# Two layers of recurrent-memory attention and gMLP on one Trainium2 core: part of the last-token projections made during the weight load

## The chip, the cores and the metric

The kernel runs on one core of one Trainium2 chip. The metric is the device time of one execution in microseconds; smaller is better. A run's time is the median of its executions. One execution is recorded by the profiler, and all views below are of that one.

## The reference

```python
def _A_ref(x, mem0, Wq, Wk, Wv, Wo, seg_len):      # 2048 tokens, 512 wide, 32 heads of 128, 8 memory rows, segments of 32
    mem = mem0
    for s in range(n_seg):                          # 64 segments, one after the other
        xs = x[:, s * seg_len:(s + 1) * seg_len, :]
        h = jnp.concatenate([mem, xs], axis=1)      # 40 rows
        q, k, v = h @ Wq, h @ Wk, h @ Wv            # per head
        p = softmax(where(mask, q @ k.T * scale, -1e9))
        o = (p @ v) @ Wo
        mem = o[:, :M, :]                           # the next segment's memory
        outs.append(o[:, M:, :])

def _B_ref(x, w_in, w_sp, b_sp, w_out):             # gMLP, 1376 wide inside, mixes over all 2048 tokens
    z = gelu(x @ w_in); z1, z2 = halves(z); z2 = layernorm(z2)
    return (z1 * (w_sp @ z2 + b_sp)) @ w_out

x = x + A(layernorm(x)); x = x + B(layernorm(x))    # twice: two layers with the same weights
x = x + A(layernorm(x)); x = x + B(layernorm(x))
```

## The kernel before

`a_block` and `b_block` run in turn, twice. The attention is a loop over 64 segments whose memory rows pass from one to the next. Four segments are a tile of 128 tokens; 16 tiles are a layer, and four tiles are a group.

A segment's 40 rows are 8 memory rows and 32 tokens. The program takes 32 of them through the segment's own chain (the 8 memory rows and the first 24 tokens: `psQ`, `psm`, `psK`, `psV` in `segment`), and does the last 8 tokens of the four segments of a tile together, 32 rows, ahead of time: query, key and value of these are the *chunks* of a tile. A chunk j is one half of the heads of Wq (j = 0, 1), Wk (2, 3) or Wv (4, 5): 16 matmuls of 128x512, four at a time in four column strips of the array (`b_mms`). Chunks go by ScalarE to `rowsB` and from there, turned by a transposing DMA on SP's queue or by VectorE (`b_out`), to `QTB` and `KTB`, or to `VB` and over DRAM (`store_v`, `spread_v`) to `VX`. GpSimd's copies in `prep_segment` take the parts of a segment from there.

The work of a chunk is put into the running tile's segments as filler: `segment` calls `fill()` three times, before `pv(0)`, before the Wo matmuls, and while VectorE makes the next memory. Each call takes one step of a generator called `more`:

- in the first four tiles of a layer `b_even` gives the next tile's six chunks as one, one and four times four matmuls a segment;
- later `b_units` gives them in nine steps over the first three segments of a tile (one, two and five times four matmuls), and the fourth segment has `y_part`: the output rows of the last tokens of the group before, 32 matmuls into `pwB`, added to `yB` by VectorE (`adds`). Rows of a whole group are stored by `store_last`.

After the attention of a segment come the output matmuls: `wo_pairs` (heads 0 to 15, two column strips a head, into `px`) and `wo_rest` (heads 16 to 31, four strips a head, into `pw`). VectorE folds `px` into `t1` by way of `cross` (`fold`), adds `pw` and turns the sum into the next segment's `hT` (`build_hA`), which the next `psQ` waits for.

PE, DVE and ACT execute in the order written inside a block (`ORDERED`); the order on SP and GpSimd is chosen by the framework's scheduler.

At the start of the first layer rows of tiles 0 and 1 and the memory are loaded on SP's queue, the weights on GpSimd's, in halves of 2048 columns: Wq and Wk first halves, second halves, Wv, Wo. Meanwhile the chunks of tile 0 and two of tile 1 are made (`units`, `units1`), in this order:

```python
units, units1 = b_units(0, 6), b_units(1, 2, alone=True)
for gen, n in ((units, 4), (units1, 2), (units, 4)):
    for _ in range(n):
        next(gen)
        run(turns)
        run(copies)
    run(turns)
```

The values of tile 0 and the rest of tile 1 are made within segment 0.

## Time and profile before

| | |
|---|---|
| time, median of 3 runs | 1623.56 us (1617.69 to 1624.75) |
| the profiled execution | 1618.1 us, its span 1616.4 us |
| TensorE busy | 1578.8 us, 98% |
| weight loads, VectorE, ScalarE, GpSimd busy | 61%, 66%, 65%, 19% |
| psQ of segments 0 and 1, first layer | 30.45 and 52.75 us |
| first layer's tile 1, tile 5 (four segments) | 38.67 and 40.12 us |
| the first layer's last segment starts | 671.4 us |

Times in the trace are counted from the span's start. A group or a timeline line tells the engine, the program's line, the operation, the tiles (out<-in), the shape and the count, and in brackets how long the engine had been idle before and what released it. `PE` are matmuls and `PEld` the loads of their stationary operand. A busy TensorE says nothing of how fast it ran; the length of equal matmuls and the granted clock do.

### The profile page before, as it was taken

Reading aid. Unit: us, or ns where it says so; the run is one execution under the profiler, and the core shown is the slowest. Engines: PE = TensorE matmul, PEld = TensorE weight load, DVE = VectorE, ACT = ScalarE, POOL = GpSimd, SP = SyncE. Lnnn points to the kernel's source line nnn. Section 1 sums busy time; section 2 is a strip of 40 time slices with the busy share of each in tenths; the row PEclk is TensorE's granted clock in tenths of the full one; section 3 lists DMA queues with packets and bytes.
Section 4 is the critical chain, followed back from the end, with each engine's and each line's share of the span. In section 5 each row is a group of like instructions: output and inputs, shape, how many; then the busy total and the mean of one; then the engine's idle time right before and its main releaser. Section 6 shows DMA issues by size and latency. Waiting matters only on the chain.

```text
span 1616.4 us, 91216 instructions
## 1 busy us (share of the span) xinstructions
PE 1578.8 (98%) x41182; PEld 983.8 (61%) x41182; DVE 1069.0 (66%) x3060; ACT 1048.9 (65%) x2281; POOL 301.6 (19%) x667
## 2 busy tenths in 40 slices
PE   5899999999999999999999999999999999999999
PEld 2566666666666766666656666666666666665565
DVE  3567766667776776784466666666677667768622
ACT  2677777777777777670047777777777777776400
POOL 5111111112211221320011111111122112224000
PEclk9999999999999999999999999999999999999999
DMA  9312121213311332377941112121233223425697
GB/s 357 100 39 46 42 43 43 44 43 85 82 47 43 90 90 70 96 181 166 210 145 44 49 43 51 46 47 47 67 92 77 47 69 99 100 52 175 145 185 171
DMA packets 259805, 148.11 MB, mean 92 GB/s; under 512 B 193752, under 2 KB 235840, under 8 KB 259416
## 3 DMA queue, kind: packets, MB, share of 16 engines
q1 hardware_dynamic: 246184, 98.46, 27.7%
q0 software_dynamic: 13232, 43.82, 8.3%
q8 instruction: 322, 5.28, 1.3%
q14 instruction: 67, 0.55, 0.1%
HBM read 59.68 MB, written 37.19 MB: 60 GB/s over the span
## 4 chain that ended last, share of the span: by engine, by line
PE 55%; DVE 1%; issue 1%; DMA 0%; ACT 0%; POOL 0%; POOLq 0%; DVEq 0%
PE pg L397 9%; PE psQ L714 7%; PE psK L714 7%; PE psb L714 5%; PE pz L296 5%; PE psO L825 3%; PE px L818 3%; PE psV L714 3%; PE psm L714 3%; PE py L440 2%; PE pwB L837 2%; PE psO L1026 2%; PE psT L1018 1%; PE psS L977 1%; PE pw L1285 0%
## 5 line engine op out<-in xcount | busy, mean ns | idle before, releaser
L714 PEld LDWEIGHTS <-hT 128*32 128x32 bf16 x12288 | 344.2, 97 | 266.5 <-DVE hT L926 12.5
L714 PE MATMUL psV<-Wv_sb,hT 128*32 128x512 bf16 x2048 | 165.8, 379 | 0.0
L954 DVE STREAM_TRANSPOSE QQ<-rows 128x256 f32<-128x256 f32 x256 | 113.1, 442 | 78.6 <-ACT rows L951 76.6
L951 ACT CAST rows<-psQ 128x512 bf16<-128x512 f32 x256 | 144.1, 591 | 29.5 <-PE psQ L714 27.3
L1047 DVE TENSOR_TENSOR uT<-psO,Rm 128x128 bf16<-128x128 f32 x256 | 74.6, 291 | 123.4 <-ACT Rm L1044 123.0
L986 ACT ACTIVATE S<-psS 128x224 bf16<-128x224 f32 x256 | 92.2, 360 | 96.9 <-PE psS L981 96.7
L954 DVE STREAM_TRANSPOSE KA<-rows 128x256 f32<-128x256 f32 x256 | 113.5, 443 | 61.7 <-ACT rows L951 58.6
L397 PE MATMUL pg<-z,wspT 128*128 128x344 bf16 x1024 | 154.3, 309 | 0.0
L1050 DVE TENSOR_TENSOR uT<-psO,Rt 128x384 bf16<-128x384 f32 x256 | 140.2, 548 | 18.7 <-ACT Rt L1126 16.4
L714 PE MATMUL psK<-Wv_sb,hT 128*32 128x512 bf16 x2048 | 151.9, 378 | 0.0
L1126 ACT ACTIVATE Rt<-Rt 128x512 f32<-128x512 f32 x256 | 147.3, 622 | 4.1
L714 PE MATMUL psQ<-Wq_sb,hT 128*32 128x512 bf16 x2048 | 136.5, 383 | 7.2 <-DVE hT L926 3.3
L825 PE MATMUL psO<-Wo_high,uT 128*32 128x128 bf16 x8192 | 140.0, 219 | 2.3 <-issue 2.0
L714 PE MATMUL psQ<-Wk_sb,hT 128*32 128x512 bf16 x2048 | 136.8, 383 | 0.0
L714 PE MATMUL psm<-Wq_sb,hT 128*32 128x512 bf16 x2048 | 135.3, 380 | 0.0
L714 PE MATMUL psK<-Wk_sb,hT 128*32 128x512 bf16 x2048 | 134.9, 379 | 0.0
L818 PE MATMUL px<-Wo,uT 128*32 128x256 bf16 x3840 | 133.2, 273 | 0.4
L1123 ACT ACTIVATE Rt<-psT 128x1024 f32<-128x1024 f32 x128 | 131.0, 1024 | 3.1
L397 PEld LDWEIGHTS <-wspT 128*128 128x128 bf16 x1024 | 100.2, 98 | 53.2
L825 PEld LDWEIGHTS <-uT 128*32 128x32 bf16 x8192 | 125.7, 97 | 8.6 <-issue 4.2
L818 PEld LDWEIGHTS <-uT 128*32 128x32 bf16 x4096 | 107.2, 97 | 27.4 <-DVE uT L1047 1.1
L911 POOL COPY KX<-old 128x128 bf16<-128x128 bf16 x128 | 65.3, 539 | 275.4 <-PE psS L981 211.0
(202 smaller groups left out, 2874.5 us busy)
## 6 DMA issues: line engine op xcount, KB each, us to landing
o_d<-o_sb SPq DMA_DIRECT2D x126, 64.0 KB
vb_d<-front SPq DMA_DIRECT2D x30, 256.0 KB
VX<-vb_d SPq DMA_DIRECT2D x120, 64.0 KB
ln_x<-xd SPq DMA_DIRECT2D x26, 256.0 KB
y_o<-o_d POOLq DMA_DIRECT2D x22, 256.0 KB, 3.4
xd<-y_o POOLq DMA_DIRECT2D x22, 256.0 KB, 2.8
Wq_sb<-in_A_Wq_dram POOLq DMA_DIRECT2D x8, 512.0 KB, 10.0
Wk_sb<-in_A_Wk_dram POOLq DMA_DIRECT2D x8, 512.0 KB, 10.4
```

The lines of the kernel that those rows point to most:

```text
L296: nc.tensor.matmul(pz[:, c0:c1], lhsT=xnT[:, kt, :], rhs=w_in_sb[:, kt, c0:c1], start=(kt == 0), stop=(kt == KT - 1))
L397: nc.tensor.matmul(pg[t][:, k, 0:344], lhsT=wsp[t][:, st, :], rhs=z(st, 344 * k, 344 * k + 344), start=(st == 0), stop=(st == NT - 1))
L714: return [nc.tensor.matmul(ps[32 * cg:32 * cg + 32, :], lhsT=lhs(kt, cg), rhs=rhs(kt, cg), start=(kt == 0), stop=(kt == KT - 1), tile_posi ...
L818: nc.tensor.matmul(px[at:at + 32, 0:256], lhsT=lhs[:, h, :], rhs=wo_rhs(h, slice(k + 2, None, -2) if h % 2 else slice(k, None, 2)), start= ...
L825: nc.tensor.matmul(pw[32 * cg:32 * cg + 32, :], lhsT=lhs[:, h, :], rhs=wo_rhs(h, cg), start=False, stop=(h == H - 1), tile_position=(0, 32 ...
L951: return r, mms, copy(r[:].rearrange("p (n el two) -> p n el two", n=8, two=2), ps.rearrange("p (n two el) -> p n el two", n=8, two=2))
L954: nc.vector.transpose(out=(QQ[:, j % 2, :, 0:32] if j < 2 else KA[:, j % 2]).bitcast(F32).rearrange("p n q one -> p n (q one)"), in_=r[:]. ...
L986: return nc.scalar.activation(out=S[:, r], in_=psS[:, r, 0:224], func=ACT.Exp, scale=scale)
L1047: nc.vector.tensor_tensor(out=hview(uT_cur[:], r, 24, 32), in0=oview(r, 0, 8), in1=Rm[:, r].rearrange("p g (n q) -> p g n q", q=8), op=ALU ...
L1050: nc.vector.tensor_tensor(out=hview(uT_nxt[:], r, 0, 24), in0=oview(r, 8, 32), in1=rview(r, 0, 24), op=ALU.mult)
L1123: nc.scalar.activation(out=Rt[:], in_=psT[:], func=ACT.Ln)
L1126: nc.scalar.activation(out=rt, in_=rt, func=ACT.Exp, scale=-1.0)
```

## The change

In the first layer chunks 0 and 2 (first half of the heads' queries and keys) of tiles 8 to 15 are taken out of the loop. The last 8 tokens of their 32 segments are two sets of 128 rows (groups 2 and 3, `EARLY`). The rows are loaded on SP's queue at the start, normalised (`early_norm`, between two steps of `_consts`), turned on TensorE (`early_turn`), and multiplied over the whole array: eight units of eight matmuls of 128x512, each copied to SBUF by ScalarE (`early_units`). The units stand between the chunks of tiles 0 and 1. GpSimd's queue stores the result to DRAM after segment 0 (`early_store`, eight DMAs). In tiles 7 to 14 of the first layer a new filler, `b_light`, gathers the next tile's two chunks by two transposing DMAs from DRAM, and spreads the four chunks left and the output rows (`y_steps`, which `y_part` now uses too) as one, one and four times four matmuls in every segment; chunk 3 is turned by VectorE. `spread_v` is issued a segment later in these tiles. In both layers `wo_pairs` takes heads 0 to 13 and `wo_rest` 14 to 31.

```diff
-WO_PAIR = 16
+WO_PAIR = 14
+EARLY = (2, 3)
+EARLY_CHUNKS = (0, 2)
...
+        for G in EARLY:
+            src = x_in[4 * P * G:4 * P * (G + 1), :].rearrange("(j r) c -> j r c", j=16)
+            nc.sync.dma_start(x_last[G], src[:, SEG - M:SEG])
...
+        def early_norm():
+            MVe, RSe = c["MVe"], c["RSe"]
+            for k, G in enumerate(EARLY):
+                _stats(nc, rp, x_last[G], MVe[:, k, :])
+            _rstd_act(nc, RSe[:], MVe[:, :, 1], c)
+            for k, G in enumerate(EARLY):
+                xn = rp.tile([P, DM], BF16, name="ln_xn", bufs=2)
+                nc.vector.tensor_scalar(out=xn[:], in0=x_last[G], scalar1=MVe[:, k, 0:1], scalar2=RSe[:, k:k + 1],
+                                        op0=ALU.subtract, op1=ALU.mult)
+                rows.early[G] = xn
...
+        def b_light(tb, G, q):
+            bs = blk_state[tb]
+            for j in EARLY_CHUNKS:
+                t = bs[("QTB", "KTB")[j // 2]][:, j % 2]
+                nc.sync.dma_start_transpose(out=t.rearrange("p (i g) k -> p i (g k)", g=4),
+                                            in_=rows.pre_d[tb // 4, j][:, tb % 4, :].rearrange("t (i e) -> t i e", i=4))
+            steps = y_steps(G, q)
+            for n, j in enumerate((4, 5, 1, 3)):
+                for _ in range(2):
+                    next(steps)
+                    yield
+                psB = accB.tile([P, 512], F32, name="psb")[:]
+                b_mms(bs, j, psB, range(KT), j == 3)
+                copies.insert(0, lambda n=n, j=j, psB=psB: b_out(bs, n % 2, j, psB, j == 3, j == 5))
+                if n == 3:
+                    next(steps, None)
+                yield
+
+        def early_turn():
+            for k, G in enumerate(EARLY):
+                pT = (att, attO[1])[k].tile([P, 2 * DM * 2], BF16, name="pT")
+                for kt in range(KT):
+                    nc.tensor.transpose(pT[:, P * kt:P * kt + P], rows.early[G][:, P * kt:P * kt + P], c["ident_bf"][:])
+                nc.scalar.copy(early_lhs(G, slice(0, KT)).rearrange("p kt (k t) -> p kt k t", t=4),
+                               pT[:, 0:KT * P].rearrange("p (kt t k) -> p kt k t", kt=KT, t=4))
...
+        def early_units():
+            stage = {}
+            for n, (j, G, k) in enumerate((j, G, k) for j in EARLY_CHUNKS for G in EARLY for k in range(2)):
+                ps = (attO[0], attO[1], att)[n % 3].tile([P, 2, 512], F32, name="psP")
+                for i in range(2):
+                    for kt in range(KT):
+                        nc.tensor.matmul(ps[:, i, :], lhsT=early_lhs(G, kt), rhs=cols_rhs(w, j, kt, 2 * k + i), start=(kt == 0), stop=(kt == KT - 1))
...
+                copies.append(lambda t=t, ps=ps: nc.scalar.copy(t, ps[:].rearrange("p a n -> p (a n)")))
+                yield stage
+
+        def early_store(stage):
+            for (G, j, k), t in stage.items():
+                nc.gpsimd.dma_start(rows.pre_d[G, j][:].rearrange("(cg k) t c -> (k t) cg c", cg=4)[:, 2 * k:2 * k + 2, :],
+                                    t.rearrange("p (cg c) -> p cg c", cg=2))
...
-            units, units1 = b_units(0, 6), b_units(1, 2, alone=True)
-            for gen, n in ((units, 4), (units1, 2), (units, 4)):
+            units, units1, early = b_units(0, 6), b_units(1, 2, alone=True), early_units()
+            stage = None
+            for gen, n in ((units, 3), (units1, 1), (None, 0), (early, 3), (units, 1), (units1, 1), (early, 2), (units, 3), (early, 3), (units, 1)):
+                if gen is None:
+                    early_turn()
...
+            light = first and tb + 1 < NB and (tb + 1) // 4 in EARLY
...
+            elif light:
+                if j4 == 0:
+                    more = b_light(tb + 1, tb // 4 - 1, tb % 4)
...
-                if j4 == (3 if first and tb == 0 else 2 if tb < 4 else 1) and tb + 1 < NB:
+                if j4 == (3 if first and tb == 0 else 2 if tb < 4 or light else 1) and tb + 1 < NB:
                     spread_v(blk_state[tb + 1])
...
             def loads():
+                if first and s == 0:
+                    early_store(stage)
```

More of the change, by code (lines that the diff above doesn't have):

```diff
@@ L52, in _ln_consts @@
     c["RS"] = [cp.tile([P, 16], F32, name=f"RS{i}") for i in range(2)]
+    c["MVe"], c["RSe"] = cp.tile([P, len(EARLY), 2], F32, name="MVe"), cp.tile([P, len(EARLY)], F32, name="RSe")
 def _identity(nc, cp):
@@ L61, in _identity, with _consts @@
     return ident_bf
-def _consts(ctx, tc, c, b_sp):
+def _consts(ctx, tc, c, b_sp, between):
     nc = tc.nc
@@ L79, in _consts @@
     nc.vector.tensor_copy(own, is_own[:].to_broadcast([P, 4, 16]))
+    between()
     for q in range(0, P, 32):
@@ L189, in __init__ @@
         self.nc, self.pool, self.xd, self.xb_d, self.o_d, self.x_in = nc, pool, xd, xb_d, o_d, x_in
-        self.xs, self.hT, self.y = {}, {}, {}
+        self.xs, self.hT, self.y, self.early = {}, {}, {}, {}
     def load(self, tb, first, eng):
@@ L520 @@
     rows.vb_d = dram.tile([P, 8 * DH], BF16, name="vb_d")
+    rows.pre_d = {(G, j): dram.tile([P, 4, 512], BF16, name=f"pre{G}{j}") for G in EARLY for j in EARLY_CHUNKS}
     with tc.manual_schedule(engines=ORDERED):
         _act_table(nc)
+        x_last = {}
         for tt in range(2):
-            x = rp.tile([P, DM], F32, name="x0", tag=("ln_x", "y_x")[tt])[:, 0:DM // 2].bitcast(BF16)
-            nc.sync.dma_start(x, x_in[tt * P:(tt + 1) * P, :])
-            rows.xs[tt] = x
+            x = rp.tile([P, DM], F32, name="x0", tag=("ln_x", "y_x")[tt])
+            rows.xs[tt] = x[:, 0:DM // 2].bitcast(BF16)
+            x_last[EARLY[tt]] = x[:, DM // 2:DM].bitcast(BF16)
+            nc.sync.dma_start(rows.xs[tt], x_in[tt * P:(tt + 1) * P, :])
         m0 = rp.tile([2 * M, DM], BF16, name="m0", tag="y_o")
@@ L547 @@
             turn(rows.m0T[:], m0[:], 2 * M)
-        _consts(ctx, tc, c, B_b_sp)
+        def early_norm():
[8 more added lines that the diff above has]
+                rows.early[G] = xn
+        _consts(ctx, tc, c, B_b_sp, early_norm)
         rest()
@@ L686, in a_block @@
                 at += n
+            oflat = v[0]
             oBr[i] = v[0].rearrange("p (h t) -> p h t", h=H)
@@ new lines, in early_lhs @@
+        def early_lhs(G, kt):
+            t = KAr[1][:].rearrange("p r n q two -> p (r n q two)").rearrange("p (g kt t) -> p g kt t", g=2, kt=KT)
+            return t[:, EARLY.index(G), kt]
+        def early_units():
[5 more added lines that the diff above has]
+                        nc.tensor.matmul(ps[:, i, :], lhsT=early_lhs(G, kt), rhs=cols_rhs(w, j, kt, 2 * k + i), start=(kt == 0), stop=(kt == KT - 1))
+                if G == EARLY[0]:
+                    at = 1024 * (2 * EARLY_CHUNKS.index(j) + k)
+                    t = oflat[:, at:at + 1024]
+                elif j == EARLY_CHUNKS[0]:
+                    t = rows.pool.tile([P, DM], F32, name=("y_x", "y_o")[k])[:].bitcast(BF16)
+                elif k == 0:
+                    t = wk.tile([P, DM], F32, name="yB", bufs=1)[:].bitcast(BF16)
+                else:
+                    t = wo.VX[1][:].rearrange("p j r e -> p (j r e)")
+                stage[G, j, k] = t
+                copies.append(lambda t=t, ps=ps: nc.scalar.copy(t, ps[:].rearrange("p a n -> p (a n)")))
+                yield stage
@@ L839, in wo_last, with y_steps @@
                 yield
-        def y_part(G, q, last=False):
+        def y_steps(G, q, last=False):
             groups = [oBs[G][:, :, 32 * g:32 * g + 32] for g in range(4)]
@@ L848, in y_part @@
             pwB = accA.tile([P, DM], F32, name="pwB")
-            for k, _ in enumerate(wo_last(parts, pwB)):
-                if k in (0, 2):
-                    yield
             def add(lo, n, src):
@@ L872, in out, with y_part @@
                     store_last(G, 0, P, nc.sync)
-            adds.append(out)
+            for k, _ in enumerate(wo_last(parts, pwB)):
+                if k == 7:
+                    adds.append(out)
+                yield
+        def y_part(G, q, last=False):
+            for k, _ in enumerate(y_steps(G, q, last)):
+                if k in (0, 2):
+                    yield
             yield
@@ L1151, in a_block @@
                 ln_turn(tb, nc.scalar.copy)
-            units, units1 = b_units(0, 6), b_units(1, 2, alone=True)
-            for gen, n in ((units, 4), (units1, 2), (units, 4)):
+            units, units1, early = b_units(0, 6), b_units(1, 2, alone=True), early_units()
[3 more added lines that the diff above has]
+                    early_turn()
                 for _ in range(n):
-                    next(gen)
+                    got = next(gen)
+                    stage = got or stage
                     run(turns)
```

## The prediction

> **What bounds the kernel now.** I read the page first (its head and the engines' shares), then the windows cut at the segments' starts, then the timeline of TensorE over the first 56 us, then the timelines of single segments on VectorE and ScalarE.

> ```profile
> span 1616.4 us, 91216 instructions
> PE 1578.8 (98%) x41182; PEld 983.8 (61%) x41182; DVE 1069.0 (66%) x3060; ACT 1048.9 (65%) x2281; POOL 301.6 (19%) x667
> ```

> TensorE is busy 98% of the span, so work taken from it should show, unless another chain is nearly as long. That is read from the first layer's tiles (four segments each, cut where psQ starts):

> ```profile
> 81.63:120.30 38.67, 38.67 (x1200) 24.22 (x1204) 26.82 (x82) 30.09 (x68) 4.20 (x9) 1.00 0.15 38
> 159.60:198.31 38.71, 38.71 (x1204) 24.03 (x1204) 27.36 (x84) 30.45 (x69) 5.92 (x15) 1.00 0.21 41
> 238.71:278.83 40.12, 40.12 (x1236) 24.72 (x1232) 27.64 (x82) 30.29 (x69) 6.49 (x15) 1.00 0.20 43
> 318.96:359.30 40.34, 40.34 (x1236) 25.95 (x1232) 27.43 (x82) 30.46 (x70) 6.87 (x16) 1.00 0.18 45
> ```

> The first columns are the stretch, its length and TensorE's busy time. Tiles 1 and 3 carry only the next tile's six chunks, spread evenly (one, one and four steps of four matmuls a segment: six steps); tiles 5 and 7 also carry the output rows (one, two, five: eight steps). Six steps cost 9.67 us a segment, eight cost 10.03. Two steps are worth 0.43 us of TensorE (16 matmuls of psb before 149.94 us last 0.86), but only 0.36 shows: at six steps the chain of the memory through VectorE ends just as the matmuls do. Segments 1 to 3 carry no spare step and still take 9.62 to 9.65. So 9.65 is a floor, and tiles 1 and 3 already sit on it.

> Before segment 0 the kernel waits for weights and runs at half speed:

> ```profile
> start us, us, engine line op out<-in xcount [idle before <-releaser]
> ...
> 13.05 0.62 PE L714 MATMUL psb<-Wq_sb,hB 128*32 128x512 bf16 x4 [0.90 <-DMA Wq_sb<-in_A_Wq_dram]
> ...
> 21.34 1.90 PE L714 MATMUL psb<-Wk_sb,hB 128*32 128x512 bf16 x16 [0.68 <-ACT rowsB L763]
> ...
> 28.56 0.40 PE L714 MATMUL psb<-Wk_sb,hB 128*32 128x512 bf16 x4 [0.87 <-DMA Wk_sb<-in_A_Wk_dram]
> 30.45 1.76 PE L714 MATMUL psQ<-Wq_sb,hT 128*32 128x512 bf16 x16 [1.49 <-DVE hT L215]
> ...
> 42.76 0.45 PE L1018 MATMUL psT<-E,ones 64*128 64x512 bf16 x4 [1.77 <-DVE E L989]
> ...
> 47.40 0.29 PE L818 MATMUL px<-Wo_high,uT 128*32 128x256 bf16 x2 [0.36 <-DMA Wo_high<-in_A_Wo_dram]
> ...
> 52.75 1.05 PE L714 MATMUL psQ<-Wq_sb,hT 128*32 128x512 bf16 x16 [1.23 <-DVE hT L926]
> ```

> Sixteen matmuls last 1.90 us at 21.34 and 1.05 at 52.75. The last weight wait costs 0.36 us; between 30.45 and 52.75 it is chiefly the chain that takes the time.

> **What it takes away.** In tiles 7 to 14 of the first layer two of six chunks and the uneven output rows become one, one, four: eight tiles from the 40.12 of tiles 5 and 6 to the 38.69 of tiles 1 and 3, 8 x 1.43 = 11.5 us. The output rows' matmuls (L837, 379 ns) are as long as the chunks' (379), so the pattern is that of tiles 1 and 3.

> **What the light tiles add.** At a light tile's end VectorE gets both the addition to yB and the turn of chunk 3; today a tile has one of them. The timeline at the start of tile 6 shows the addition, then the transposes that the scores wait for:

> ```profile
> 280.42 0.68 DVE L854 TENSOR_TENSOR yB<-pwB,yB 128x512 f32<-128x512 f32 x1
> 281.02 0.43 DVE L954 STREAM_TRANSPOSE QQ<-rows 128x256 f32<-128x256 f32 x1
> 281.40 0.45 DVE L954 STREAM_TRANSPOSE KA<-rows 128x256 f32<-128x256 f32 x1
> ```

> The turn (0.70, next start 0.63 later, at the start of tile 3) moves the KA transpose to 282.03, its end to 282.48. Scores(0) come 3.67 us after psQ (143.94 after 140.27), here 282.50, and want KA some 0.13 earlier (243.45 to 243.58): a stall of about 0.1, 8 x 0.1 = +0.9 us with what it drags. Bounds: 0, since the two ends nearly meet, and 8 x 0.4 = 3 if the last copy of a tile comes late as well.

> The gathers are free while they have time: two transposing DMAs from DRAM, issued at a tile's first filler, read by POOL's copies in its last segment, some 25 us later. The nearest row, the front's transposes of twice the size from xb_d, lands in 2.2 to 3.8 us. On SP they take 1.23 us each, and a light tile issues three transposes in place of four; behind them stand stores of o_sb that nobody awaits for tiles. Without that cover POOL's KX and QQ copies would come late by as much as the gather. ScalarE loses two copies a tile, off the path.

> **Wo pairs to 14 heads.** From the first px matmul to the first of L825 is 0.873 us for 16 heads, from there to the next matmul 0.894: 54.6 against 55.9 ns a head. Two heads moved cost 2.6 ns in 127 segments, +0.3 us. px being ready 0.11 us earlier lets VectorE add px and cross earlier, but memT waits for psO afterwards (0.21 us idle, `PE psO L825`), and the heads still run in order. Bounds: -1 (where VectorE came late) to +1.2 (matmuls of 59 ns, as 0.95 us from 148.13 to 149.08 would make them).

> **The start.** 64 matmuls of 512 columns over the whole array. Price by column from L296 in the chain's list (`687.58 37.44 PE pz L296 x256`, 16 tiles x 4 x 1376 columns): 0.425 ns, so 0.218 us each, 13.9 us at full speed, the same as what 16 chunks cost later (16 x 0.86). The steps: tile 0's chunk 0 ends at 13.67, plus 0.6 for two more loads of 128 KB ahead of weights that arrive at 410 GB/s: 14.3. Tile 1's chunk 0 needs the same PSUM tile, so the copy first (0.7), then 1.90: 16.9. Eight transposes (0.58 for four) and two copies of 0.59, partly overlapped: 18.2. Their input is ready: the new statistics, scales and two ScalarE steps end near 12.5 on VectorE, and push the mask's copies by 1.5 us into time that VectorE has (1.45 idle at 14.40). Three early units, 24 matmuls: 5.2, plus the half-speed part, 1.7: 25.1. Chunk 2 of both tiles 1.8, two units 3.5, chunk 1 0.9, three units 5.2, chunk 3 0.9: 37.4. ScalarE's copies (1.02 per 128x1024, as L1123) stay under a unit's 1.74. The handover by VectorE took 1.49 and a last long copy stands ahead: 1.7, psQ at 39.1 in place of 30.45. From there at full speed chunk 4's copy comes after 4.55 in place of 6.29 (five groups of 16 at 0.87 and 0.2); the 6.02 of VectorE's chain to psT stay; the 9.99 from psT to segment 1 lose some 0.5 with the wait for Wo_high. Segment 1 starts at 59.1 in place of 52.75: +6.3 us. Bounds: 0 (the weights hide it all) to +11 (half speed for 9 us more, or the gathers' stores ahead of Wo in POOL's queue).

> The eight stores cost POOL 8 x 0.54 us (L224's row) behind its copies for segment 1; they wait for copies long done, and the next copies for segment 2 have 9 us.

> [...] The trace holds one recorded stretch of half clock, 30.64 to 34.05, after a stretch in which TensorE was busy 0.99 of 3.42 us; it cannot show what transposes count for. [...]

> **Sum**, on the profiled execution's 1618.1 us (span 1616.4 and 1.7 around it): -11.5 + 0.9 + 0.3 + 6.3 = -4.0, so 1614.1. The three timed runs spread from 1617.69 to 1624.75 with their median 5.5 above that execution; -4.0 on 1623.56 is 1619.6. 0.5%, about what a measurement of this kernel can tell from no change, is 8.1 us.

> **Rivals.** (1) The early block is hidden altogether. TensorE idles some 10 us between 10 and 30.45, and the last weights arrive at 47.4, whatever it does. If the start costs 0 to 2 us, the sum is -10.3 to -8.3: 1613 to 1615. Against it: TensorE needs 13.9 us plus its own chunks after 14.3, and segment 0 is a chain on VectorE, not a wait for weights.

> (2) Slower: the clock is not granted in the early block. Matmuls ran at half speed until about 27 us although TensorE was busy 63% of 20.39 to 23.81. If the short gaps between units and copies keep it so, the 64 matmuls cost 12.2 more than summed above (13.9 less the 1.7 already in), five chunks 4.3, and segment 0 its 1.7 again: the start costs 6.3 + 18.2 = 24.5, the sum is +14.2, 1638. It decides where the start's cost passes 18.4 us, which makes the sum +8.1. Against: after 81% of 23.81 to 27.22 the matmuls at 28.56 took 0.40 and not 0.62, and the early units leave smaller gaps. [...]

> (3) The tiles gain nothing, since gathers or turns hold the scores: a late gather of 1.4 us a tile eats the 11.5, and the sum is +7.5, 1631. Landing times speak against it.

> **Numbers.** The forecast, within 0.5%, has 0.66; rival 1 with milder forms 0.21; rival 2, and rival 3 with a dearer start, past the threshold 0.13. Taking the bounds together (-11.5 - 1 + 0 + 0 to -11 + 3 + 1.2 + 11), with the runs' spread, 1611 to 1630 holds eight in ten.

> **What would show it.** Segments of tiles 7 to 14 at 9.67 to 9.70 us, the first segment after each light tile 0.1 longer; segment 0 at 38 to 40 us and segment 1 at 58 to 60; layer two unchanged within 1 us; early units 1.74 us each from 24 us on. It is wrong if light segments stay over 9.8, if segment 1 starts before 55 or after 64, or if half-speed matmuls last past 28 us.

## The result: 0.5% slower, and the profile after

The changed kernel takes 1630.27 us (median of 7 executions, 1627.01 to 1632.06), the kernel before 1623.37 beside it (7 executions, 1617.69 to 1625.04). The ratio is 1.0052, with a 95% interval of 1.0038 to 1.0066: slower by some 8.4 us by that ratio and 6.9 between the two medians, where 4 us less were forecast. The median lies 0.3 us beyond the upper end of the range. (The ratios below leave out one execution: 9136 us, of the kernel before with 128 more instructions, whose eleven others took 1622 to 1631.)

The head and the engines' shares of the page after, and its line on the queue that brings the program's code (packets, MB, share of 16 engines' span):

```profile
span 1625.3 us, 91887 instructions
PE 1586.1 (98%) x41510; PEld 984.7 (61%) x41510; DVE 1073.5 (66%) x3074; ACT 1055.0 (65%) x2277; POOL 307.7 (19%) x675
...
q8 instruction: 325, 5.32, 1.4%
```

The span is 8.9 us longer. The windows after, for tiles 1, 5, 7 and 8 of the first layer, of which 7 and 8 are now light (the columns are stretch, length, TensorE's busy time, and on):

```profile
89.05:127.99 38.94, 38.94 (x1216) 23.73 (x1216) 26.89 (x82) 30.05 (x68) 4.38 (x9) 1.00 0.16 38
247.46:287.76 40.30, 40.30 (x1252) 24.83 (x1248) 27.48 (x83) 30.48 (x70) 6.97 (x16) 1.00 0.18 45
329.59:369.28 39.69, 39.41 (x1222) 24.34 (x1215) 26.35 (x80) 28.71 (x64) 5.44 (x12) 1.00 0.16 40
369.28:408.56 39.28, 39.28 (x1220) 26.54 (x1220) 29.84 (x92) 30.01 (x69) 8.40 (x20) 1.00 0.35 75
```

The light tiles (the last two lines) are shorter than 40.1, but not 38.7; and tile 1, in whose fillers nothing was changed, has grown from 38.67 to 38.94. TensorE's timeline at the start:

```profile
18.82 6.99 PE L875 MATMUL psP<-Wq_sb,KA 128*128 128x512 bf16 x24 [1.23 <-ACT KA L861]
...
32.12 5.35 PE L875 MATMUL psP<-Wk_sb,KA 128*128 128x512 bf16 x24
...
39.94 1.05 PE L737 MATMUL psQ<-Wq_sb,hT 128*32 128x512 bf16 x16 [1.49 <-DVE hT L219]
...
50.56 0.45 PE L1106 MATMUL psT<-E,ones 64*128 64x512 bf16 x4 [1.77 <-DVE E L1077]
...
59.85 1.05 PE L737 MATMUL psQ<-Wq_sb,hT 128*32 128x512 bf16 x16 [1.51 <-ACT Rt L1211]
```

Segment 0 starts at 39.94 for 30.45, segment 1 at 59.85 for 52.75.

To see where the 8.9 us lie I cut both executions at the segments' starts and took each class's median and what its segments take beyond that median, in sum:

| class | before, us | after, us |
|---|---|---|
| layer one, segments 1 to 3 (no spare steps) | 9.62 | 9.72 |
| layer one, tiles 1 to 3 (six steps) | 9.67 | 9.77 |
| layer one, tiles 4 to 6 (eight steps) | 10.03 | 10.06 |
| layer one, tiles 7 to 14 (light after) | 10.04 | 9.79 |
| layer two, tiles 0 to 3 / 4 to 15 | 9.76 / 10.03 | 9.75 / 10.04 |
| beyond the medians, all segments | 9.1 in all | 16.7 in all |

The start adds 7.1; the 32 light segments take off 32 x 0.25 = 8.0; the other medians add 2.2; what lies beyond the medians adds 7.6; the rest is 0.1. That is 9.0 of 8.9. The third of these terms stood in my sum at 0.3, the fourth not at all. In layer two's tiles 0 to 3 this execution of the kernel before is no measure: its median of 9.76 is a high one, for eight other executions with 16 heads (in the experiments) have 9.67 to 9.69 there, and the six with 14 heads, this one after among them, 9.75 to 9.81.

### The profile page after: what moved, and what is told of

Same layout as the page of the kernel before. It is cut to its first block, busy times and chain, and to the rows that moved or that the text cites. A ratio compares the mean times of both kernels' runs of the same rounds, so it can differ in the third digit from the quotient of the medians.

```text
span 1625.3 us, 91887 instructions
## 1 busy us (share of the span) xinstructions
PE 1586.1 (98%) x41510; PEld 984.7 (61%) x41510; DVE 1073.5 (66%) x3074; ACT 1055.0 (65%) x2277; POOL 307.7 (19%) x675
## 3 DMA queue, kind: packets, MB, share of 16 engines
q8 instruction: 325, 5.32, 1.4%
## 4 chain that ended last, share of the span: by engine, by line
PE 93%; DVE 2%; DMA 2%; issue 2%; ACT 1%; POOL 1%; SPq 0%; POOLq 0%; DVEq 0%; ACTq 0%
PE psQ L737 13%; PE psK L737 13%; PE psb L737 9%; PE pg L401 9%; PE psO L907 8%; PE psm L737 6%; PE psV L737 6%; PE px L900 6%; PE pz L300 5%; PE pwB L919 3%; PE psO L1114 3%; PE py L444 2%; PE psT L1106 2%; PE psS L1065 2%; PE psP L875 1%
## 5 line engine op out<-in xcount | busy, mean ns | idle before, releaser
L907 PE MATMUL psO<-Wo_high,uT 128*32 128x128 bf16 x8704 | 148.5, 219 | 4.2 <-issue 4.2
L907 PEld LDWEIGHTS <-uT 128*32 128x32 bf16 x9216 | 143.4, 97 | 14.1 <-issue 6.8
L900 PE MATMUL px<-Wo,uT 128*32 128x256 bf16 x3584 | 120.8, 273 | 0.7 <-DVE uT L1135 0.2
L999 POOL COPY KX<-front 128x128 bf16<-128x128 bf16 x126 | 63.7, 537 | 271.0 <-PE psS L1069 152.6
```

The lines of the kernel that those rows point to most:

```text
L900: nc.tensor.matmul(px[at:at + 32, 0:256], lhsT=lhs[:, h, :], rhs=wo_rhs(h, slice(k + 2, None, -2) if h % 2 else slice(k, None, 2)), start= ...
L907: nc.tensor.matmul(pw[32 * cg:32 * cg + 32, :], lhsT=lhs[:, h, :], rhs=wo_rhs(h, cg), start=False, stop=(h == H - 1), tile_position=(0, 32 ...
L999: eng.tensor_copy(KX[r][:].rearrange("p g (k i) -> p i g k", i=4), bs["KTB"][:, r].rearrange("p (i g) k -> p i g k", i=4)[:, :, :, 8 * j4: ...
```

## The experiments

Ratios are to the kernel before, run on the same chip (its medians there are 1623.2 to 1624.5), with the 95% interval. A recorded execution is one sample of many: times of the kernel before run from 1617.7 to 1631.8.

**The change once more**, unedited, to see which parts of its trace repeat.

> The changed kernel once more, unedited. Theory A (a cause fixed in the program): 1629 to 1631 us again, the floor segments at 9.72 us, and TensorE's waits put down to issue, 7.8 us in the first profile, come back at the same places. Theory B (chance of one execution): the time or the places of these waits move by more than 2 us.

1633.56 us, 1.0059 [1.0041, 1.0078], some 2.5 us above what theory A had. The classes repeat (9.73, 9.75, 10.06, 9.79). The waits put down to issue didn't repeat in sum: 12.3 us in 29 places for 7.8 in 16, so theory B holds for them (more of this below). Nor did the start: segment 1 came at 60.81, with segment 0 partly at half clock, in two such stretches of which this is the first:

```profile
48.20:51.61 3.41, 2.51 (x34) 1.29 (x35) 1.34 (x6) 0.59 (x2) 0.94 (x2) 0.50 1.02 386
```

(The 0.50 is the granted clock.)

**The changed kernel with 16 heads in pairs, and the kernel before with 14.**

```diff
-WO_PAIR = 14        # the changed kernel
+WO_PAIR = 16
```
```diff
-WO_PAIR = 16        # the kernel before
+WO_PAIR = 14
```

> The changed kernel with WO_PAIR = 16 again. Theory A: wo_rest writes into the tile psO[1], which VectorE's memory_out(1) still reads, so it can't start before that read ends, however few heads come first; the two moved heads then stand behind that end, 0.11 us in each segment that is bound by the memory's chain. Undone, segments 1 to 3 go from 9.72 to 9.62, tiles 1 to 3 and the light tiles from 9.73-9.79 to 9.67-9.70, segments of eight steps stay at 10.03: 63 segments of 0.06 to 0.10, 4 to 6 us less than the changed kernel (1624 to 1626). The prediction's step (2.6 ns in every segment): 0.3 us less, floor segments unchanged.

> The kernel before with WO_PAIR = 14 and nothing else. Theory A (the wait on psO[1]): segments 1 to 3 from 9.62 to 9.72, tiles 1 to 3 and the second layer's tiles 0 to 3 up by 0.06 to 0.1, segments of eight steps unchanged at 10.03: 31 segments, +2 to +3 us. The prediction's step: +0.3 us over all segments alike.

Sixteen heads in the changed kernel: 1619.69 us, 0.9988 [0.9971, 1.0005]. Fourteen in the kernel before: 1633.11 us, 1.0056 [1.0037, 1.0076]. The constant that I priced at 0.3 us moves either kernel by 9 to 12 us, where theory A had 4 to 6 and 2 to 3. With 16 the segments 1 to 3 are back at 9.62 and tiles 1 to 3 at 9.67; with 14 the kernel before has 9.72 and 9.74. So the term sits in the segments at the floor, as theory A has it. Eight-step segments mostly hide it: with 14 the kernel before has medians of 10.04 in tiles 7 to 14 and 10.05 in layer two, but 10.16 in tiles 4 to 6.

The timelines of one such segment show how. Before:

```profile
69.88 0.29 DVE L1047 TENSOR_TENSOR uT<-psO,Rm 128x128 bf16<-128x128 f32 x1 [0.60 <-ACT Rm L1044]
70.12 0.28 PE L818 MATMUL px<-Wo_high,uT 128*32 128x256 bf16 x2
70.22 0.90 PEld L825 LDWEIGHTS <-uT 128*32 128x32 bf16 x64
70.23 1.08 PE L825 MATMUL psO<-Wo_high,uT 128*32 128x128 bf16 x64
...
71.36 0.29 DVE L924 TENSOR_TENSOR memT<-psO,t 128x128 bf16<-128x128 f32 x1 [0.23 <-PE psO L825]
```

After:

```profile
66.82 0.95 PE L900 MATMUL px<-Wo,uT 128*32 128x256 bf16 x28
...
67.36 0.29 DVE L1135 TENSOR_TENSOR uT<-psO,Rm 128x128 bf16<-128x128 f32 x1 [0.27 <-ACT Rm L1132]
67.48 1.24 PEld L907 LDWEIGHTS <-uT 128*32 128x32 bf16 x72
67.71 0.24 PE L907 MATMUL psO<-Wo,uT 128*32 128x128 bf16 x4
67.77 1.13 PE L907 MATMUL psO<-Wo_high,uT 128*32 128x128 bf16 x68
...
68.95 0.29 DVE L1012 TENSOR_TENSOR memT<-psO,t 128x128 bf16<-128x128 f32 x1 [0.45 <-PE psO L907]
```

`wo_rest` writes `pw` into the tile `psO` that VectorE still reads for the second half of `uT`. Before, that read ends at 70.17 and the matmul starts 0.06 later; after, it ends at 67.65 and the matmul again starts 0.06 later. The after lines show it best: the weight load of head 14 runs at 67.48, since its `uT` has long been there, and its matmul waits until 67.71. In the lines of before the tile can't be told from another cause: heads 16 to 31 read the half of `uT` that the same VectorE operation writes. After, heads 14 and 15 have their half since 66.76 and wait all the same. So `wo_rest` starts when that read ends, however few heads stand ahead of it: over layer one's floor segments from the first `px` matmul to the first of `wo_rest` it is 0.88 to 0.92 us in both, with 32 `px` matmuls or 28. From there to the start of its last matmul it grew from 0.86 to 0.97 us, and VectorE's `memT`, the next memory, waits for its end. Two heads moved behind the wait are 0.11 us a segment there. Putting `pw` somewhere else in PSUM was not tried; by the above it could free heads 14 and 15, not the later ones.

**Eighteen heads in pairs, both kernels.** If only the wait counted, more heads ahead of it would be better.

```diff
-WO_PAIR = 14        # the changed kernel; from 16 in the kernel before
+WO_PAIR = 18
```

> The changed kernel with WO_PAIR = 18. Theory A (the wait of wo_rest on the read of psO[1]): 16 heads fill that wait exactly, so two more in front change nothing there; px ends 0.11 us later and VectorE's fold has 0.24 us to spare, so segments 1 to 3 stay at 9.62 and the light tiles at 9.67 to 9.78 as with 16. Theory F (late code): 8 TensorE instructions a segment fewer than with 16, in its densest stretch; the sum of what segments take over their class median falls from 14.8 us by 2 to 5, and the time to 1615 to 1618. Rival to both: the fold comes last, and floor segments go up by 0.05 to 0.1 (1622 to 1625).

> The kernel before with WO_PAIR = 18. Theory A: class medians 9.62, 9.67, 10.03 as before. Theory F: with 8 instructions a segment fewer the sum over the medians stays at or under the 9.1 us of before (where it was small already), time 1619 to 1623. Rival (the fold comes last): +2 to +3 us from 31 floor segments.

1625.25 us, 1.0008 [0.9994, 1.0021], and 1626.4 us, 1.002 [1.001, 1.003]. Segments 1 to 3, which carry no filler, stay at 9.62, but tiles 1 to 3 go to 9.80 in both. The timeline of one floor segment of the kernel before with 18:

```profile
69.69 0.29 DVE L1047 TENSOR_TENSOR uT<-psO,Rm 128x128 bf16<-128x128 f32 x1 [0.60 <-ACT Rm L1044]
69.92 0.41 PE L818 MATMUL px<-Wo_high,uT 128*32 128x256 bf16 x6
...
70.16 0.96 PE L825 MATMUL psO<-Wo_high,uT 128*32 128x128 bf16 x56
```

The two heads more didn't come ahead of the wait: heads 16 and 17 are in the half of `uT` that this VectorE operation writes, and in every floor segment of layer one exactly their four `px` matmuls start after it. `px` is complete 0.13 us later after that operation than with 16, while `wo_rest` ends as before. The rival holds: the later `px` delays VectorE's fold, and the third filler, whose `psb` stands in the PSUM tile that the fold reads, comes 0.13 us late. So 16 is the number of heads whose `uT` is there ahead of the wait; fewer lengthen what stands behind it, more delay the fold.

**Twelve in the kernel before**, the other way.

```diff
-WO_PAIR = 16
+WO_PAIR = 12
```

> The kernel before with WO_PAIR = 12. Theory A (wo_rest's first matmul waits for the read of psO[1], which ends at a fixed time): segments 1 to 3 at 9.83 (+0.11 for two heads more behind the wait), tiles 1 to 3 at 9.84 to 9.88, and segments of eight steps start to grow too (their slack of 0.26 less 0.22): 10.03 to 10.08. Theory F: 8 instructions more a segment, so the sum over the medians grows again. Together 1638 to 1645. The prediction's step: 0.7 us over before.

1642.88 us, 1.011 [1.0091, 1.0128]: segments 1 to 3 at 9.86, tiles 1 to 3 at 9.88, another 0.14 above the 9.72 and 9.74 of 14 heads. The mechanism holds in size, with 0.11 expected; but 31 floor segments at 0.1 are only 3 us, and the total moved by more each time. Here the eight-step segments rose as well, beyond the 10.03 to 10.08 expected: medians of 10.26 in tiles 4 to 6, 10.16 in tiles 7 to 14 and 10.20 in layer two, in sum some 15 us. Something else moves with the constant.

**Code that comes late.** By the waits of after TensorE stands on "issue", that is on nothing that the profile shows, for 7.8 us in 16 places, for 2.6 us in 8 before (idle times over 0.1 us). Waits of TensorE, before:

```profile
PE psO L825 <- issue: 2.0, 5, 0.6
```

After:

```profile
PE psO L907 <- issue: 4.2, 8, 1.3
...
PE psQ L737 <- issue: 1.7, 4, 0.6
PE pwB L919 <- issue: 1.4, 2, 0.7
```

Counting TensorE's instructions from the start (loads, matmuls and some 220 that wait for semaphores or drain), every one of these stalls, in both kernels, stands at a load whose number is 193 modulo 256, or at its matmul, the next. It ends 1.2 to 1.6 us (one of them 2.0) after a packet of the instruction queue has ended; 5.32 MB in 325 packets are 16.4 KB each. The count gives 83,238 such instructions after and 82,583 before, or 325 and 322 times 256, which is the number of packets in each. By that count one packet goes with 256 of TensorE's instructions, a block in what follows. The second execution of the changed kernel stalls again at 14 of the 16 places, and at 15 more. One of the 14, after:

```profile
508.54 0.61 PE L737 MATMUL psQ<-Wq_sb,hT 128*32 128x512 bf16 x8 [0.52 <-issue]
```

The same program again:

```profile
511.84 0.61 PE L737 MATMUL psQ<-Wq_sb,hT 128*32 128x512 bf16 x8 [0.56 <-issue]
```

So many places belong to the program's layout, while the sum differs by 4.5 us between two executions of one program. To see what the layout is worth, I pushed the blocks along by small transposes into a spare tile at the start, each a load and a matmul, 128 or 64 instructions, and left all else:

```diff
+PAD = 64            # 32 in the second pair
...
+            pad = turn_ps.tile([P, KT * 2 * M], BF16, name="pad", tag="turn")
+            for i in range(PAD):
+                nc.tensor.transpose(pad[:, 0:2 * M], m0[:, 0:P], c["ident_bf"][0:2 * M, 0:2 * M])
```

The kernel before, and with 14 heads, moved by 128:

> The kernel before with 64 small transposes (128 TensorE instructions) that nothing reads, at 9 to 13 us while weights load; they move all later TensorE instructions by half of a 16 KB block of code (256 instructions). Theory F (waits put down to issue are late code, and depend on how blocks fall on the segments): class medians 9.62, 9.67 and 10.03 stay, the start costs under 1 us, but the waits (2.6 us in the profile of before, 7.8 in that of the changed kernel) move to other places and their sum changes by some us, and the time by as much, either way. Theory D (they come from the changed kernel's own DMAs): sum and places as before, time within 1 us.

> The kernel before with WO_PAIR = 14 and the 128 extra TensorE instructions at the start. If the part of e2's loss beyond the floor segments (9 us lost, some 3 of them there) is an accident of where code blocks fall, shifting the blocks changes it: below 1629 or above 1637, and other places. If it comes with 14 heads itself (8 more TensorE instructions a segment in its densest stretch), it stays: 1631 to 1635.

The same moved by 64:

> The kernel before with 64 extra TensorE instructions (a quarter of a block). With before (1623.4) and e3 (1626.8) a third point of the 16-head kernel's spread over block positions: 1620 to 1628, class medians unchanged.

> The kernel before with 14 heads and 64 extra TensorE instructions: a third point beside e2 (1633.1) and e9 (1628.7). If 14 heads cost about 3 us in the floor segments and the rest is the accident of blocks, the three 14-head points lie 3 to 5 us above the three 16-head points on average; if 14 heads bring more late code by themselves, 6 to 9 us above.

The changed kernel moved by 128:

> The changed kernel (14 heads) with 128 extra TensorE instructions at the start, which shift its code blocks by half a block. If its 14 us against e1 come from 14 heads as such, it stays at 1629 to 1634. If a part is the accident of its blocks (as between e2, 1633.1, and e9, 1628.7), it falls to 1624 to 1628 or rises above 1636; at most 4 us (the floor segments) are then owed to the heads.

| ratio to before | as it is | moved by 128 | moved by 64 | mean |
|---|---|---|---|---|
| before, 16 heads | 1 | 1.0018 [1.0002, 1.0034] | 1.0028 [1.0015, 1.0042] | 1.0015 |
| before, 14 heads | 1.0056 [1.0037, 1.0076] | 1.0027 [1.0013, 1.0041] | 1.0053 [1.0032, 1.0074] | 1.0045 |
| changed | 1.0052 [1.0038, 1.0066] | 1.0035 [1.002, 1.0051] | | |

The medians of layer one's floor classes are untouched by the shifts (9.62 and 9.67 to 9.68 with 16 heads, 9.72 and 9.74 to 9.75 with 14). The whole moves all the same: by 0.2 and 0.3% with 16 heads (1626.77 and 1628.72 us, the second a little above what was expected), by 0.3% and not at all with 14 (1628.71 and 1632.98 us). The changed kernel's 1629.82 us is in the range expected if its loss belongs to its 14 heads, and its two intervals overlap. The stalls on issue of the recorded executions moved too, 2.6, 5.9 and 9.1 us with 16 heads and 8.9, 7.2 and 6.5 with 14, in the order of the columns; but each is one execution, and with 14 they don't follow the times. The kernel before stands in the most fortunate of its three positions. Over the three, 14 heads cost 0.30% (0.56, 0.09 and 0.25% by position), 4.9 us, of which the floor segments explain some 3; with a scatter between positions nearly as large, the size is known to a few us only, the sign by the timelines.

**The start alone**: 16 heads, early units made, and no light tiles.

```diff
-WO_PAIR = 14
+WO_PAIR = 16
...
-            light = first and tb + 1 < NB and (tb + 1) // 4 in EARLY
+            light = False
```

> The changed kernel with WO_PAIR = 16 and without the light tiles: the early block and its stores are made and not used, all chunks stay in the tiles. Measures the start by itself. The prediction's step: segment 1 starts at 59 to 61.5 us in place of 52.75 (+6.3 to +8.8), segments of tiles 7 to 14 at 10.03 as before, the time 1629 to 1632. Rival (the early block is hidden, and the missing gain lies in the tiles): 1623 to 1625.

1627.7 us, 1.0028 [1.0015, 1.0042], segment 1 at 60.94; segment 0 is 22.35 us long in place of the 19.91 after, again with two stretches at half clock (the 16 matmuls at 50.32 and at 52.91 take 1.90 us each time, for 1.05 at full clock). The time is under the 1629 to 1632 expected and over the rival's 1625: the start alone costs 0.28%, 4.5 us. Against 0.9988 with light tiles the light tiles give 0.40%, 6.5 us. Both kernels ran in one position of the code only, so these sizes are known to some 0.2 to 0.3%.

**One group early**, half the units, for tiles 12 to 15 only.

```diff
-EARLY = (2, 3)
+EARLY = (3,)
-... (early, 3), (units, 1), (units1, 1), (early, 2), (units, 3), (early, 3), (units, 1)):
+... (early, 2), (units, 1), (units1, 1), (early, 1), (units, 3), (early, 1), (units, 1)):
```

(With 16 heads, as in all that follow.)

> The changed kernel with WO_PAIR = 16 and EARLY = (3,): half of the early block (four units), light tiles 11 to 14 alone. If start and gain both scale, the start costs 3.5 to 4.5 us (segment 1 at 56 to 57) and the tiles give 4 x 1.3 = 5.2 less some 0.5: 1621 to 1623, as e1 within 2 us. If the first units are cheaper than the last (they lie in waits), the start costs 2 or less: 1619.

1621.77 us, 0.999 [0.9979, 1]. TensorE's timeline of that start:

```profile
27.75 1.05 PE L738 MATMUL psb<-Wk_sb,hB 128*32 128x512 bf16 x16
...
30.28 1.05 PE L738 MATMUL psQ<-Wq_sb,hT 128*32 128x512 bf16 x16 [1.49 <-DVE hT L219]
```

Segment 0 starts at 30.28 and segment 1 at 52.03, as before or a little sooner: four units cost nothing, since they replace idle time, and the full clock comes at 19.67 in place of 27.22 (a chunk takes 1.05 us at 24.93, where before one took 1.90 at 23.92). In these executions all of the start's price is in the second four. The time, though, is 1621.77 where 1619 was expected for a start that costs nothing; the difference is no larger than what a position moves.

**The last unit in the hand-over**, behind chunk 3, where TensorE waited 1.49 us for VectorE.

```diff
-... (units, 3), (early, 3), (units, 1)):
+... (units, 3), (early, 2), (units, 1), (early, 1)):
```

> The changed kernel with WO_PAIR = 16 and the last early unit moved behind chunk 3, into the 1.5 us in which TensorE waits for VectorE's turn before psQ. Theory: the start's cost is TensorE time that finds no wait to lie in (four units cost nothing in e7, eight cost 7 to 9); this one finds a wait, so segment 0 starts 1.4 to 1.7 us earlier than in e1 (37.5 to 38 us) and the time is 1618 or so, 1 to 2 under e1. Rival (ScalarE's long copy or the PSUM tile holds segment 0): no gain.

1618.99 us, 0.9979 [0.9962, 0.9997], the lowest ratio so far, with an interval that overlaps the 0.9988 of its neighbour without the move. Its timeline:

```profile
35.55 1.90 PE L875 MATMUL psP<-Wk_sb,KA 128*128 128x512 bf16 x7
...
37.38 1.05 PE L737 MATMUL psQ<-Wq_sb,hT 128*32 128x512 bf16 x16
```

The first psQ follows with no idle time, 2.56 us earlier than after and 1.84 earlier than in the neighbour (39.22), segment 1 at 57.29. Its tile 8, for the 39.28 of after:

```profile
363.84:402.91 39.07, 39.07 (x1205) 24.22 (x1205) 30.13 (x92) 29.92 (x69) 8.40 (x20) 1.00 0.31 75
```

Moved by 128 instructions as above:

> e8 (16 heads, last early unit in the handover) with the same shift. If e8's 4.4 us under the kernel before are owed to its work, it stays at 1617 to 1621; if they are the luck of its blocks, 1622 to 1627.

1618.26 us, 0.9954 [0.9939, 0.9969]: in both positions it is faster than the kernel before as it stands, by 0.2 and 0.5%.

**What keeps the light segments above 9.67.** With 16 heads they are 9.67 without and 9.77 with row work of VectorE (`spare2`, statistics of the rows just finished). The timeline of one, with 16 heads:

```profile
394.90 0.42 DVE L151 BATCH_NORM_STATS2 bnst<-y_o 128x6 f32<-128x256 f32 x1
...
395.35 0.28 DVE L1005 COPY cross<-px 64x128 f32<-64x128 f32 x1
...
395.73 0.29 DVE L1007 TENSOR_TENSOR t<-px,cross 128x128 f32<-128x128 f32 x1
...
396.08 1.05 PE L737 MATMUL psb<-Wq_sb,hB 128*32 128x512 bf16 x16
```

The statistics stand ahead of the fold, and the third filler follows the fold's last read of `px`. I moved the row work behind the fold; this kernel also holds 16 heads and the last unit in the hand-over, so its neighbour is the kernel above.

```diff
+            def spare3():
                 for y, added in ys:
...
-            def spare3():
```

> The changed kernel with WO_PAIR = 16 and spare2's part of the row work (a half addition or half statistics, 0.3 to 0.4 us of VectorE) moved behind the next memory, into spare3. Theory G: in the light tiles the third step's matmuls write the PSUM tile that fold has just read (accB), and this work delays fold by 0.1; so segments of light tiles with row work take 9.77 where others take 9.67. Moved, they go to 9.67 to 9.70 (18 segments, 1.5 to 2 us), unless the later token outputs then hold the next segment's scores (9.8 or more). Rival (the 0.1 comes from somewhere else): 9.77 stays.

1621.64 us, 0.998 [0.9968, 0.9991]. Many of the segments did fall to 9.67, so the 0.1 is due to that order. But the first segments of tiles 9, 10 and 14, 9.90 to 10.04 in the neighbour, now take 10.25 to 10.43, and the second ones of tiles 8, 9, 10 and 13 take 10.6 to 10.8. TensorE's timeline in the first of tile 9 and the second of tile 8:

```profile
406.60 0.28 PE L1065 MATMUL psS<-QQ,KA 128*32 128x40 bf16 x16 [0.38 <-DVE KA L1042]
```
```profile
380.42 0.55 PE L907 MATMUL psO<-Wo_high,uT 128*32 128x128 bf16 x25
...
381.84 0.52 PE L907 MATMUL psO<-Wo_high,uT 128*32 128x128 bf16 x23 [0.86 <-issue]
```

In the first kind the scores wait 0.30 to 0.38 us for VectorE's `KA`, which comes behind the moved work, as the expectation allowed for. In the second kind TensorE has one idle time of 0.8 to 0.9 us, put down to issue in three of the four, and in tile 9 to VectorE's `uT`, held up by a row's load; these are not shown to come from the move. As it stands, moving the work gives nothing.

## Why the prediction was wrong, step by step

Against its sum of -4.0 the profile has +8.9, a miss of 12.9: the start 0.8, the light tiles 2.6, the other segments' medians 1.9, and 7.6 beyond the medians.

- *The start, +6.3.* Measured +7.1. The units took 6.99 for the 6.9 put together there, psQ came at 39.94 for 39.1, psT 10.62 after it for 10.57, segment 1 at 59.85 for 59.1. In other executions half clock falls into segment 0 and makes it 8.1 to 8.8. The rival of a half-speed early block (1638) did not come about. What transposes count for with the granted clock cannot be told here, since the full clock came at 22.17 with other work about (the units' matmuls last 624 ns in the mean from 18.82 to 22.1, 391 from 22.3 to 25.7). The rival of a free start is half true: four units were free, eight were not. One reading was wrong: the trace before holds a second stretch of half clock beside 30.64 to 34.05, from 829.36 to 832.77 in layer two's first segment (granted clock 0.50). After has none there (1.00), and that segment takes 10.02 us for 11.41: luck of 1.4 us on the side of the change.
- *The light tiles, -11.5 + 0.9.* The medians give -8.0, at 9.79 for the 9.67 to 9.70 forecast (9.78 with 16 heads). The step that failed took tiles 1 and 3 as the pattern because the fillers' matmuls are equal. Those tiles have no row work on VectorE just ahead of the fold (`spare2`), many segments of light tiles have, and the third filler waits for the fold. I had priced what comes at a tile's end, which is mostly there (with 16 heads the first segment after a light tile takes 9.76 to 9.78 where no row work adds to it, once 9.68), and left out what stands inside the segments. Rival 3, tiles that gain nothing because gathers or turns hold the scores, did not come about: the tiles do gain.
- *Wo pairs to 14, +0.3.* This is the step that failed outright. "The heads still run in order" misses that `wo_rest` waits for VectorE's read of its PSUM tile: its start is fixed by that read, so heads moved behind it lengthen the chain by their whole time, 0.11 us, of which 0.05 to 0.10 shows in each floor segment, not by the 2.6 ns a segment of the sum, and the upper bound of +1.2 shared the flaw. The timeline before gave a hint: psO's matmul starting at 70.23, 0.06 us after a VectorE operation on psO ends. The medians outside the light tiles rose by 2.2, of which 1.5 is layer one's floor segments. By the average of three positions of the kernel before 14 heads cost about 5, with an uncertainty of a few us. "Layer two unchanged within 1 us" failed as well (+1.7, with the luck of 1.4 in it).
- *What the sum had no term for.* Code that comes late: TensorE's stalls on "issue" grew by 5.2 us between the two recorded executions, beside the 7.6; by the second execution of the changed kernel they grew by 9.7. The shifts show that position alone can move this kernel by 0.2 to 0.3%, as much as the whole forecast. How much of the 7.6 belongs to the changed layout and how much to these two executions isn't settled; nor is what makes a given block late.

Without the constant the changed kernel stands at 0.9988, 1.9 us below the kernel before with an interval that takes in both no change and the forecast of -4.0; so the start and the light tiles were roughly right together, and the third edit turned the sign. The evidence is that the five versions with 16 heads and light tiles lie at 0.9954 to 0.999, and both positions of the changed kernel with 14 at 1.0035 and above. By how much it did so is less sure, since the version with 16 heads and no other edit ran in one position only.

## What to carry to other kernels

Before moving work across a point in an engine's order, ask what the instruction at that point waits for, its output tile's last reader included: work moved from ahead of a fixed wait to behind it can cost its whole time, however small the difference in price (here 0.11 us a segment, priced at 2.6 ns). A pattern taken from another stage holds only if every engine's work in it is the same, not the matmuls alone. And where an edit is worth half a per cent or less, run it in two or three positions of the code, by a few harmless instructions at the start, before believing its sign.
